# Moving one accumulating transfer ahead of two others in GpSimd's queue (gated mix of an S5 scan and an H3 convolution)

## The chip, the cores and the metric

The kernel runs on one core of a Trainium2 chip. A core has five instruction streams: TensorE (PE, matrix products into PSUM), VectorE (DVE), ScalarE (ACT), GpSimd (POOL) and SyncE (SP), and 16 DMA engines that serve the transfers issued from these streams. The metric is the time on the device in microseconds (us), as the median of several runs.

## The reference

Two branches share the input x (2048 steps, 1024 channels) and are mixed by a gate. Branch A is a diagonal complex state-space recurrence (S5); branch B shifts and multiplies two inputs and convolves the product with one long filter per channel, by FFT (H3).

```python
def _A_ref(x, Lambda_re, Lambda_im, B_re, B_im, C_re, C_im, log_dt, Dskip):
    dt = jnp.exp(log_dt)
    Lam_bar = jnp.exp(dt * Lam)
    B_bar = ((Lam_bar - 1.0) / Lam)[:, None] * Bmat
    Bu = jnp.einsum("bld,pd->blp", x + 0j, B_bar)
    for t in range(L):
        h = Lam_bar[None, :] * h + Bu[:, t, :]
        hs.append(h)
    y = 2.0 * jnp.einsum("blp,dp->bld", hseq, Cmat).real + x * Dskip[None, None, :]

def _B_ref(q, k, v, shift_k, ssm_k, ssm_D):
    for t in range(ks):                       # ks = 4 taps
        k_shift = k_shift + k_pad[:, t:t + S, :] * shift_k[:, ks - 1 - t][None, None, :]
    kv = k_shift * v
    y = irfft(rfft(kv padded) * rfft(ssm_k padded))[:S]
    y = y + kv * ssm_D[None, None, :]
    return q * y                              # q is x

g = sigmoid((x * gate_w).sum(-1, keepdims=True))
return g * a + (1 - g) * b
```

## The kernel before

The program is one unrolled list of instructions per engine; small helpers (`mm`, `tt`, `ts`, `act`, `move`, `gather`, lines 92 to 127) append each instruction to its engine's list in exactly the order of the calls, so an engine executes what the source names in that order, and waits by semaphore where its data or its buffer is not ready. `gather` is a DMA issued from POOL that adds its source to its destination; `move` and `load_t` are issued from SP. Since all helpers record their instructions at one place, nearly every instruction of the profile stands at line 94.

Branch B comes first. The 1024 channels are cut into eight groups of 128, and a loop over c = 0 to 6 (line 1136) works on three groups at a time: group c + 2 is loaded and gets its four taps, group c + 1 is transformed, group c is multiplied, and group c - 1 is transformed back. The pieces are generators; `step` runs one up to its next `yield`, `run` to its end. Those that matter here:

- `products(c)` (line 680) multiplies the spectra of filter (K) and signal (V) block by block on DVE. After its second product, `n1` into the tile `wkh`, it issues `gather(G[:, :, 1:], n1)`, 768 KB that are added into the spectrum G (line 708); a later step on DVE, `tt(G[:, :, 2:], G[:, :, 2:], n1, ALU.add)` (line 726), reads and writes G again.
- `times_v(c + 1)` (line 593) multiplies the tap sums `ks` by v, mirrors them on PE, takes a difference on DVE into `ev` and issues `gather(ks[:, 2:4], lo)`, 256 KB (line 606). `fwd_V` (line 667) reads `ev` and then `ks` on PE.
- `turn_table(c - 1)` (line 461), for c = 1 to 4, makes a piece of the tables `TC`, `TS` of cosines and sines with which branch A's scan later turns its states. It has three parts: four ACT instructions write two halves of the tile `hr` (float32 `h`, int32 `n`); `gather(h, n)` adds the second half to the first, 256 KB (line 470); three ACT instructions take the absolute value, sine and cosine. In the loop the third part comes one pass later: the generator is kept as `old`, and the next pass begins with `step(old)`.
- `inverse(c - 1)` (line 738) reads G on PE, and SP stores the result.
- `taps(c + 2)` (line 563) multiplies on PE the transposed input `kT` and a rearranged copy `kB`, which SP's transfers `spread` (line 224) prepare from c = 3 on.

Alongside, PE begins with the products of branch A (`Bu`, the generator `parts`). The tiles `hr` and the products' `t` share one pool of three buffers (`u4`, line 83). Behind the loop come the last groups of branch B, and then branch A's scans on DVE, its output products on PE and the mix with branch B.

Of the kernel before, what the change touches and what calls it, by code (L numbers as in the profile page):

```python
# [20 lines left out]
def kernel(  # L21
# [158 lines left out]
    def hold(column):  # L180
        act(column, pih, func=ACT.Copy)

    def by_channel(c):
        return c == 0 or 3 <= c < NC - 1

    def load(which, c, held=False):
        cc = slice(c * 128, (c + 1) * 128)
        if which == "kn":

            if by_channel(c):  # L190
                t = ld.tile([128, S], BF16, name="kn", tag="ld")
                move(t, B_ssm_k[cc, :])
            else:
                t = ld.tile([128, NT, 128], BF16, name="kn", tag="ld")
                load_t(t, B_ssm_k[cc, :])
        elif which == "v":

            w = 2 if c == 2 else 1
            if c == NC - 1:
                t = ld.tile([128, NT, 128], BF16, name="v", tag="ld")  # L200
            elif c == 2:
                lds["v2"] = xt_pool.tile([128, NT, 2, 128], BF16, name="v2", tag="xT")
            if c < 2:
                t = ld.tile([128, NT, 128], BF16, name="v", tag="ld")
            elif c < NC - 1:
                t = lds["v2"][:, :, c % 2:c % 2 + w].rearrange("p n k d -> p n (k d)")
            if held:
                hold(t[:, 0, 0:1])
            move(t, vf.rearrange("(n p) d -> p n d", p=128)[:, :, c * 128:(c + w) * 128])
            for k in range(w):  # L210
                lds["v", c + k] = t[:, :, k * 128:(k + 1) * 128]
            return
        else:

            t = ld.tile([128, PAD + S], BF16, name="kT", tag="ld")
            put("pool", nc.gpsimd.memset, t[:, 0:PAD], 0.0)
            if held:
                hold(t[:, PAD:PAD + 1])
            load_t(t[:, PAD:], kf[:, cc])
            if c >= 3:  # L220
                lds["kB", c] = ld.tile([128, PAD + S], BF16, name="kB", tag="ld")
        lds[which, c] = t

    def spread(c):

        a, b = lds["kT", c], lds["kB", c]
        lo, hi, n = slice(0, 64), slice(64, 128), PAD + S
        move(b[lo, 8:], a[hi, 8:])
        move(b[hi, 10:], a[hi, 8:n - 2])
        yield  # L230
        move(a[hi, 10:], a[lo, 8:n - 2])
# [13 lines left out]
    def load_BT(g, c, held=False):  # L245
        if held:
            hold(BT[g][:, c, 0, 0:1])
        load_t(BT[g][:, c], (A_B_re, A_B_im)[c][g * 256:(g + 1) * 256, :])

    def load_xT(tb, halves=(0, 1), held=False):  # L250
        if tb not in xTs:
            xTs[tb] = (xt_pool if tb in (1, 2) else xt_first).tile([128, ND, TB], BF16, name="xT", tag="xT")
        for h in halves:
            if held:
                hold(xTs[tb][:, 0, h * HB:h * HB + 1])
            load_t(xTs[tb][:, :, h * HB:(h + 1) * HB], xf[tb * TB + h:(tb + 1) * TB:2, :])
# [306 lines left out]
    def taps(c, dg):  # L563
        kT, kB = lds.pop(("kT", c)), lds.pop(("kB", c), None)
        ks = ks_pool.tile([128, 4, 4, 128], BF16, name="ks")
        for h in range(2):
            sums = tap_sums(kT, dg, h) if c < 3 else packed_sums((kT, kB), dg, h)
            act(of_blocks(ks, h), by_block(sums), func=ACT.Copy)
        kss[c] = ks
# [59 lines left out]
    def fwd_K(c, fis=range(NFI)):  # L629
        eo = eos["k", c]  # L630
        if c not in KH:
            KH[c] = spectrum("K", c)
        for fi in fis:
            fsl = slice(fi * 128, (fi + 1) * 128)
            ps = ps2([128, 2, 4, 128], "psk")
            for cc in range(2):
                tab = CF if cc == 0 else SF
                for mt in range(2):
                    mm(ps[:, cc], tab[:, mt, fsl], eo[:, cc, mt], mt == 0, c == NC - 1 and mt == 1)
                for mt in range(0 if c == NC - 1 else 2):  # L640
                    tb2 = (SF, NCF)[cc][:, mt, fsl]
                    mm(ps[:, cc, 1:4], tb2, eo[:, 1 - cc, mt, 0:3], False, mt == 1)
            act(of_tile(KH[c], fi), ps, func=ACT.Copy)
# [423 lines left out]
    def step(gen):  # L1067
        next(gen, None)

    def run(gen):  # L1070
        for _ in gen:
            pass

    def steps(gen, n):
        for _ in range(n):
            step(gen)
# [59 lines left out]
    for c in range(NC - 1):  # L1136
        n, nn = c + 1, c + 2
        if c == 0:
            load("kn", 2)
            load("kT", 2)  # L1140
            load("v", 2)
            load_BT(0, 0)
            load_xT(0, (0,))
            p1 = products(0, 1)
            fwd_K(n, (0, 1))
            step(p0)
            run(tv)
            dg = dgs(nn, True)
            steps(p1, 2)
            step(p0)  # L1150
            step(p1)
            run(p0)
            taps(nn, dg)
            step(sp)
            fwd_K(n, (2, 3))
            step(p1)
            step(sp)
            fwd_V(n)
            run(p1)
            run(fold_K(nn))  # L1160
            tv = times_v(nn)
            step(tv)
            load("kn", 3)
            load("kT", 3)
            load_BT(0, 1)
            apart = spread(3)
            step(apart)
            load_xT(0, (1,))
            run(apart)
            lam_diag(0, lam_pool, True)  # L1170
            continue
        if c == 6:
            put("pool", nc.gpsimd.tensor_copy, stamp, xTs[2][:, 0, 0:HB + 1:HB])
        tabs, back, prod = turn_table(c - 1) if c <= NG else none, inverse(c - 1), products(c)
        step(old)
        step(tabs)
        if c == 6:
            step(parts)
        step(back)
        step(tv)  # L1180
        steps(prod, 3)
        run(tv)
        step(old)
        step(tabs)
        run(back)
        run(old)
        fk = none
        if nn < NC:
            dg = dgs(nn)
            if by_channel(nn):  # L1190
                fk = fold_columns(nn)
                step(fk)
        if c == 2:
            step(parts)
        fwd_K(n, (0, 1))
        if c in (2, 6):
            step(parts)
        fwd_K(n, (2, 3))
        if c == 4:
            step(parts)  # L1200
        if c == 6:
            run(sp)
            s5p["Q"] = s5p["wu"]
            run(turns_U[2])
            gate(0)
        step(prod)
        if nn < NC:
            if not by_channel(nn):
                fk = mirror_K(nn)
            step(fk)  # L1210
            if c < 5:
                step(fk)
            if c == 4:
                step(parts)
            if c == 1:
                load_BT(1, 0, True)
            elif c < 5:
                load("v", nn, True)
            step(parts)
            taps(nn, dg)  # L1220
            if c == 5:
                load("v", nn)
                load_xT(2, held=True)
            if nn + 1 < NC:
                load("kT", nn + 1, True)
                load("kn", nn + 1)
                apart = spread(nn + 1)
                step(apart)
                if c == 1:
                    load_BT(1, 1)  # L1230
                elif c in (2, 3):
                    load_xT(1, (3 - c,))
                run(apart)
        step(prod)
        run(fk)
        run(prod)
        if n == NC - 1:
            overlap_K(n)
        if nn < NC:
            tv = times_v(nn)  # L1240
            step(tv)
            step(parts)
        else:
            run(next(tiles))
            CT[0] = ld.tile([128, 2, D], BF16, name="CTa", tag="ld")
            hold(CT[0][:, 0, 0:1])
            load_CT(0)
            load_BT(2, 0)
            load_BT(2, 1)
            run(next(tiles))  # L1250
            run(next(tiles))
        fwd_V(n, (0, 1))
        if c < 6 and c != 4:
            step(parts)
            if c in (1, 3):
                step(parts)
        fwd_V(n, (2, 3))
        if c in (4, 5):
            step(parts)
        if c == 1:  # L1260
            lam_diag(1, lam_pool)
        old = tabs
# [284 lines left out]
```

## Time and profile before

| what | value |
|---|---|
| median of 3 runs | 382.79 us (381.41 to 388.19) |
| profiled execution | 381.05 us |
| its span, first to last instruction | 379.3 us |
| PE busy | 372.4 us (98% of the span) |
| DVE busy | 369.3 us (97%) |
| ACT busy | 309.1 us (81%) |
| POOL busy | 81.2 us (21%) |
| TensorE clock granted, mean | 0.998 |
| loop passes c = 1 to 4 | about 45.9 to 139 us |

The span is one execution as the hardware profiler recorded it. The times of a table of instructions are in us from its start. A transfer has two times: its issue, which is an instruction of the issuing engine, and its landing, which the rows of the DMA issues give in us from the issue. POOL's instructions include those issues; a name such as `G<-wkh` reads "G written from wkh".

### The profile page before, as it was taken

The numbers are of one execution on the slowest core, as the hardware profiler recorded it, in microseconds if no ns is written. First come the engines' busy times: TensorE is split into PE (matmuls) and PEld (weight loads), VectorE is DVE, ScalarE is ACT, GpSimd is POOL, SyncE is SP. The second block draws the span as 40 slices with busy tenths as digits, with TensorE's granted clock in tenths as the row PEclk, the third lists the DMA queues.
The fourth block names the chain that finished last, engine by engine and source line by source line (L and its number), as shares of the span: only waits on it lengthen the run. The fifth ranks groups of instructions, "written<-read, shape, count | busy, mean of one in ns | idle before, by whom it ended". The sixth has DMA issues, their size and how long they took to land.

```text
span 379.3 us, 6708 instructions
## 1 busy us (share of the span) xinstructions
PE 372.4 (98%) x2469; PEld 200.1 (53%) x2469; DVE 369.3 (97%) x595; ACT 309.1 (81%) x475; POOL 81.2 (21%) x111
## 2 busy tenths in 40 slices
PE   7999999999999999999999999999999999999996
PEld 5656357575674846644454444444445444444444
DVE  8899999999999999999999999999999999999996
ACT  5879997988979999786949999996989759937611
POOL 4011030110301103031003112122414323635000
PEclk9999999999999999999999999999999999999999
DMA  7979999999999998969998999957898999899902
GB/s 168 168 115 242 234 202 193 232 209 202 194 170 213 233 207 177 174 144 152 199 200 188 200 230 257 250 111 134 155 231 174 221 251 246 145 250 164 225 2 111
DMA packets 126547, 71.78 MB, mean 189 GB/s; under 512 B 104681, under 2 KB 107633, under 8 KB 126514
## 3 DMA queue, kind: packets, MB, share of 16 engines
q1 hardware_dynamic: 112416, 45.90, 55.7%
q0 software_dynamic: 12976, 25.17, 39.2%
q10 hardware_dynamic: 1122, 0.28, 0.5%
q8 instruction: 19, 0.31, 0.3%
q14 instruction: 14, 0.11, 0.1%
HBM read 15.48 MB, written 8.39 MB: 63 GB/s over the span
## 4 chain that ended last, share of the span: by engine, by line
DVE 42%; PE 27%; DMA 14%; issue 10%; ACT 4%; POOL 2%; SPq 0%; DVEq 0%; POOLq 0%; ACTq 0%
PE both L94 16%; DVE BT L94 12%; DMA U<-Q 10%; DVE wkh L94 8%; DVE G L94 5%; DVE W L94 3%; PE psk L94 3%; PE psz L94 2%; DMA V<-Q 2%; DVE t L94 2%; DVE ks L94 2%; DVE hb L94 2%; PE psv L94 2%; PE taps L94 1%; DMA kT<-in_B_k_dram 1%
## 5 line engine op out<-in xcount | busy, mean ns | idle before, releaser
L94 PEld LDWEIGHTS <-BT 128*128 128x128 bf16 x640 | 62.1, 98 | 48.3 <-issue 0.2
L94 PE MATMUL both<-xT,BT 128*128 128x512 bf16 x384 | 83.7, 379 | 0.0
L94 POOL DMA_DIRECT2D U<-Q x26 | 26.4, 1029 | 82.3 <-ACT Q L94 40.5
L94 PEld LDWEIGHTS <-hb 128*128 128x128 bf16 x256 | 25.0, 98 | 30.2 <-issue 0.5
L94 PEld LDWEIGHTS <-U 128*128 128x128 bf16 x252 | 24.6, 98 | 27.4
L94 PE MATMUL psy<-CT,hb 128*128 128x512 bf16 x160 | 36.8, 379 | 0.0
L94 ACT ACTIVATE Vh<-psv 128x1024 bf16<-128x1024 f32 x32 | 30.7, 1032 | 5.8 <-PE psv L94 5.8
L94 PE MATMUL psy<-CT,U 128*128 128x512 bf16 (+1 forms) x160 | 35.1, 368 | 0.0
L94 ACT ACTIVATE U<-both 128x512 bf16<-128x512 f32 x44 | 24.2, 594 | 10.0 <-PE both L94 9.7
L94 DVE TENSOR_TENSOR_SCAN W<-rv,init,A 128x256 bf16<-128x256 f32 x48 | 32.1, 729 | 0.0
L94 POOL DMA_DIRECT2D G<-wkh x8 | 9.8, 1219 | 102.6 <-DVE wkh L94 102.6
L94 ACT ACTIVATE Q<-U,lam 128x512 bf16<-128x512 bf16 (+1 forms) x52 | 29.9, 612 | 0.0
L94 PE MATMUL psk<-eok,SF 128*128 128x384 bf16 (+1 forms) x120 | 28.5, 354 | 0.0
L94 PEld LDWEIGHTS <-SF 128*128 128x128 bf16 x184 | 18.0, 98 | 18.8 <-issue 0.2
L94 PE MATMUL psz<-G,CI 128*128 128x512 bf16 x64 | 24.3, 379 | 0.0
L94 PE MATMUL psz<-G,SI 128*128 128x512 bf16 x64 | 24.3, 379 | 0.0
L94 PE MATMUL psy<-CTa,hb 128*128 128x512 bf16 x96 | 22.7, 379 | 0.0
L94 PE MATMUL taps<-dg,kT 128*128 128x128 bf16 (+1 forms) x352 | 21.7, 210 | 0.7 <-DMA kT<-in_B_k_dram 0.6
L94 PEld LDWEIGHTS <-kT 128*128 128x128 bf16 x352 | 21.1, 100 | 2.3 <-DMA kT<-in_B_k_dram 1.8
L94 DVE TENSOR_TENSOR wkh<-BT,Vh 128x3072 bf16<-128x3072 bf16 (+4 forms) x20 | 21.8, 1109 | 0.0
L94 DVE TENSOR_TENSOR wkh<-Kh,Vh 128x3072 bf16<-128x3072 bf16 (+2 forms) x16 | 21.3, 1349 | 0.0
L94 PE MATMUL psy<-CTa,U 128*128 128x512 bf16 (+1 forms) x92 | 20.8, 370 | 0.0
(230 smaller groups left out, 843.5 us busy)
## 6 DMA issues: line engine op xcount, KB each, us to landing
U<-Q POOLq DMA_DIRECT2D x26, 256.0 KB, 5.1
G<-wkh POOLq DMA_DIRECT2D x6, 768.0 KB, 8.8
cv_scr<-cv SPq DMA_DIRECT2D x16, 256.0 KB, 7.7
kn<-in_B_ssm_k_dram SPq DMA_DIRECT2D x5, 512.0 KB, 4.4
v<-in_B_v_dram SPq DMA_DIRECT2D x5, 512.0 KB, 7.1
out_dram<-m SPq DMA_DIRECT2D x8, 256.0 KB, 4.2
BT<-cv_scr SPq DMA_DIRECT2D x7, 256.0 KB, 6.6
out_dram<-BT SPq DMA_DIRECT2D x7, 256.0 KB, 2.0
```

Of the source, the lines that this page charges most:

```text
L94: i = f(*a, **kw)
```

## The change

In the loop, `step(tabs)`, which issues `gather(h, n)`, moves up by four calls. It stood behind `run(tv)`, that is behind the transfer into `ks`; it now stands ahead of `steps(prod, 3)`, that is ahead of the transfer into G. Both orders come after the first `step(tabs)`, whose ACT instructions write `hr`. It concerns the passes c = 1 to 4; in the passes 5 and 6 `tabs` is empty.

```diff
         step(back)
         step(tv)
+        step(tabs)
         steps(prod, 3)
         run(tv)
         step(old)
-        step(tabs)
         run(back)
         run(old)
```

The lists of PE, DVE, ACT and SP keep their instructions and their order. In POOL's list each of the four passes changes from

```
G<-wkh, ks<-lo, hr<-hr
```

to

```
hr<-hr, G<-wkh, ks<-lo
```

and the clearing of a few columns of the next `kT`, which POOL does in each pass behind these, keeps its place behind `ks<-lo`. POOL's instruction for `hr<-hr` now carries a wait on ACT's writes of `hr` itself; before, waits of earlier POOL instructions had covered it.

## The prediction

> **What bounds the kernel now.** I read the page's first line, then a table of busy time over the stretch in which the moved transfer occurs, 45.9 to 139 us: four passes of the channel loop, c = 1 to 4.
>
> ```profile
> span 379.3 us, 6708 instructions
> ```
>
> ```profile
> core 0: us, PE busy (x) PEld busy (x) DVE busy (x) ACT busy (x) POOL busy (x), PEclk, DMA share, GB/s
> 45.90:139.00 93.10, 92.54 (x801) 59.62 (x802) 92.69 (x84) 84.12 (x134) 12.38 (x16) 1.00 1.07 206
> ```
>
> Of 93.10 us PE is idle for 0.56 and DVE for 0.41, at full clock. Both are full at once, so no order of transfers can take more than about half a microsecond out of these passes, while a transfer that comes late for either of them lengthens the pass at once. The DMA engines are full too (share 1.07). POOL has 12.38 us of work: its own time is worth nothing, the moments at which its transfers land are all that matters. So I follow three transfers per pass, all in POOL's queue.
>
> **The order and the landings before.** First POOL's instructions in order of time (start, duration, instruction, and in brackets what it waited for), then for the four passes in turn the rows of the DMA issues (size, and us from issue to landing).
>
> ```profile
> 50.07 1.20 POOL L94 DMA_DIRECT2D G<-wkh  x1 [14.72 <-DVE wkh L94]
> 52.88 0.91 POOL L94 DMA_DIRECT2D ks<-lo  x1 [1.61 <-DVE ev L94]
> 53.45 1.22 POOL L94 DMA_DIRECT2D hr<-hr  x1
> ...
> 74.06 1.20 POOL L94 DMA_DIRECT2D G<-wkh  x1 [18.18 <-DVE wkh L94]
> 76.87 0.90 POOL L94 DMA_DIRECT2D ks<-lo  x1 [1.61 <-DVE ev L94]
> 77.43 1.22 POOL L94 DMA_DIRECT2D hr<-hr  x1
> ...
> 97.07 1.20 POOL L94 DMA_DIRECT2D G<-wkh  x1 [15.90 <-DVE wkh L94]
> 99.88 0.90 POOL L94 DMA_DIRECT2D ks<-lo  x1 [1.61 <-DVE ev L94]
> 100.44 1.23 POOL L94 DMA_DIRECT2D hr<-hr  x1
> ...
> 120.08 1.20 POOL L94 DMA_DIRECT2D G<-wkh  x1 [17.11 <-DVE wkh L94]
> 122.89 0.90 POOL L94 DMA_DIRECT2D ks<-lo  x1 [1.60 <-DVE ev L94]
> 123.44 1.23 POOL L94 DMA_DIRECT2D hr<-hr  x1
> ```
>
> ```profile
> ks<-lo POOLq DMA_DIRECT2D x1, 256.0 KB, 8.4
> hr<-hr POOLq DMA_DIRECT2D x1, 256.0 KB, 11.1
> ```
>
> ```profile
> ks<-lo POOLq DMA_DIRECT2D x1, 256.0 KB, 7.2
> hr<-hr POOLq DMA_DIRECT2D x1, 256.0 KB, 8.5
> ```
>
> ```profile
> ks<-lo POOLq DMA_DIRECT2D x1, 256.0 KB, 7.9
> hr<-hr POOLq DMA_DIRECT2D x1, 256.0 KB, 11.6
> ```
>
> ```profile
> ks<-lo POOLq DMA_DIRECT2D x1, 256.0 KB, 8.8
> hr<-hr POOLq DMA_DIRECT2D x1, 256.0 KB, 9.9
> ```
>
> Start plus landing time gives when ks is complete: 61.28, 84.07, 107.78 and 131.69 us; and hr: 64.55, 85.93, 112.04 and 133.34. The difference is what hr takes behind ks: 3.27, 1.86, 4.26 and 1.65 us, on average 2.76. Against those landings stand the first uses. The rows are the first matmul pair on ks in each pass, the first and the last of the four additions into G on DVE, and the landing times of the four G transfers (shortest, median, longest).
>
> ```profile
> 62.04 0.59 PE L94 MATMUL psv<-ks,SF 128*128 128x512 bf16 x2
> ...
> 87.24 0.59 PE L94 MATMUL psv<-ks,SF 128*128 128x512 bf16 x2
> ...
> 109.04 0.59 PE L94 MATMUL psv<-ks,SF 128*128 128x512 bf16 x2
> ...
> 133.94 0.59 PE L94 MATMUL psv<-ks,SF 128*128 128x512 bf16 x2
> ```
>
> ```profile
> 61.77 1.23 DVE L94 TENSOR_TENSOR G<-G,wkh 128x2048 bf16<-128x2048 bf16 x1
> ...
> 131.77 1.23 DVE L94 TENSOR_TENSOR G<-G,wkh 128x2048 bf16<-128x2048 bf16 x1
> ```
>
> ```profile
> DMA to landing us min/median/max: 8.8/8.9/9.2
> ```
>
> ks has 0.76, 3.17, 1.26 and 2.25 us to spare. G was used 11.70 us after its issue in the first pass and 11.69 in the last; with the longest landing, 9.2, that leaves 2.49 to spare. Neither made anyone wait. hr has more than that: its next reader is the ScalarE instruction below, 3.86 us after the landing at 64.55.
>
> ```profile
> 68.41 0.63 ACT L94 ACTIVATE hr<-hr 128x512 f32<-128x512 f32 x1
> ```
>
> **The change, part by part.** No instruction is added or removed. One POOL issue per pass with its 256 KB DMA moves, from behind ks to ahead of G. PE, DVE, ACT and SP keep their order.
>
> *What it removes.* hr no longer stands last in POOL's queue. Nobody waited for it there, and PE and DVE have 0.56 and 0.41 us of idle time in all; worth between 0 and 0.56 us, taken as 0, because hr lands well ahead of its reader.
>
> *The wait on POOL.* hr must now wait for ScalarE to have written both halves of it, with G's issue queued behind on POOL, and ks behind G. The last writes are these; POOL's lag after a release is read from the DVE row, whose product ends at 49.78 while G's issue starts at 50.07: 0.29 us.
>
> ```profile
> 47.26 0.90 ACT L94 ACTIVATE hr<-row,nthn 128x256 int32<-128x256 f16 x2
> ...
> 70.86 0.90 ACT L94 ACTIVATE hr<-row,nthn 128x256 int32<-128x256 f16 x2
> ...
> 94.43 0.93 ACT L94 ACTIVATE hr<-row,nthn 128x256 int32<-128x256 f16 x2
> ...
> 117.86 0.89 ACT L94 ACTIVATE hr<-row,nthn 128x256 int32<-128x256 f16 x2
> ```
>
> ```profile
> 48.03 1.75 DVE L94 TENSOR_TENSOR wkh<-Kh,Vh 128x3072 bf16<-128x3072 bf16 x1
> ```
>
> They end at 48.16, 71.76, 95.36 and 118.75; with the lag, hr is issued at 48.45, 72.05, 95.65 and 119.04, ahead of G's old starts by H = 1.62, 2.01, 1.42 and 1.04 us. hr's issue takes 1.22 us, so only in the last pass can G be pushed on POOL itself, by up to 0.19 us. hr's own issue comes 5.00, 5.38, 4.79 and 4.40 us earlier than before.
>
> *The queue of the DMA engines.* In every pass G, ks and hr landed in the order of issue, so I take POOL's queue as first in, first out: hr's 256 KB are now served before G. If hr needs S us of service, it delays G and then ks by D = S - H. S is not shown at this place. From below: 1.65 us, the smallest of the four spacings; from above 4.26, the largest. I take the mean, 2.76. Then D is 1.14, 0.75, 1.34 and 1.72 us. G's 2.49 us cover all of it. ks's cover holds in the second and fourth pass and falls short by 1.14 - 0.76 = 0.38 and 1.34 - 1.26 = 0.08 in the first and third: PE then waits in front of the ks matmuls, everything of PE behind it, and DVE's next products soon after. Sum: 0.46 us, put down as **0.5 us slower**. With S = 1.65 the sum is 0. With S = 4.26, D is 2.64, 2.25, 2.84 and 3.22; ks is late by 1.88, 0, 1.58 and 0.97 = 4.43 us, and G by 0.15, 0, 0.35 and 0.73 at most, which lies beside the same stalls for the most part; I take 5 us as the end.
>
> The Trainium skill, "DMA: Bandwidth & Descriptors", section "Anatomy of one DMA — SWDGE (gpsimd) path", gives about 2.0 us fixed plus bytes over 436 GB/s for such a transfer, by which 256 KB occupy the engines for an estimated 0.6 us: the sum by it is 0. The spacings of 1.65 to 4.26 us say that this queue never gets the engines alone here.
>
> *Neighbours in the other queue.* hr now moves while SP's transfers for the next taps do. The tightest one is in the fourth pass:
>
> ```profile
> 121.21 0.47 SPq L94 DMA_DIRECT2D kT<-kT  x1
> ```
>
> ```profile
> kT<-kT SPq DMA_DIRECT2D x1, 256.8 KB, 7.4
> ```
>
> ```profile
> 129.90 0.22 PE L94 MATMUL taps<-dg,kT 128*128 128x64 bf16 x2
> ```
>
> It landed at 128.61, 1.29 us ahead of the taps. What POOL's queue takes more than before is the head start H, 1.04 us in this pass, so even a delay of that length would still be covered: 0.
>
> **The sum.** It is made against the profiled execution, 381.05 us (379.3 of span and 1.75 around it). The median of the runs shown is 382.79, 1.74 above it, with runs from 381.41 to 388.19; the new kernel will be measured by such runs too, so I add to the median: 382.79 + 0.5 = **383.3 us**. Something like 2% (7.7 us) is what a measurement of this kernel can tell from no change.
>
> **The rivals.**
>
> 1. *ks late in earnest, still inside 2%.* If each pass keeps its own spacing (3.27 and 4.26 in the first and third), D is 1.65 and 2.84, and ks is late by 0.89 and 1.58: 2.5 us, 385.3. A middle value comes from the share of the engines:
>
> ```profile
> q0 software_dynamic: 560, 1.31, 34.3%
> ```
>
> In the first pass (45.9 to 69 us) POOL's queue filled 34.3% of the 16 engines, 7.92 us for 1280 KB, so 1.58 us per 256 KB. If the other queue is full as well and the two take turns, S is twice that, 3.17; D is 1.55 and 1.75 in the passes that matter, and ks is late by 0.79 and 0.49: 1.3 us, 384.1. That the engines take turns between queues packet by packet is the rule of the Trainium skill, same page, "Queues, rings and completion order"; no row here shows single packets. For this rival: the DMA share of 1.07. Against: G landed within 8.8 to 9.2 us in all passes, whatever was beside it.
>
> 2. *Slower by more than 2%: hr holds the head of the queue.* Place: hr's transfer of 32-bit words, in front of G in POOL's queue. Price: with S = 5.3 us, D is 3.7, 3.3, 3.9 and 4.3, ks is late by 2.9, 0.1, 2.6 and 2.0, together 7.7 us: 390.5. From S = 5.3 on it decides, and each further microsecond costs four. For it: hr's 11.1 and 11.6 us to landing are the longest of the three transfers. Against: most of that is waiting behind ks, and no spacing exceeds 4.26.
>
> 3. *Faster.* POOL's queue is empty 1.7 to 4.3 us sooner in each pass, so the next loads of SP go undisturbed. The gain is capped by PE's 0.56 us of idle time: 382.2. More than 2% faster would need a stretch in which PE and DVE are not full; this one has none.
>
> 4. *The change moves nothing.* If ScalarE wrote hr later than DVE finishes the product for G, hr's issue would sit at G's place and hold G back. The writes end 1.3 to 2.3 us ahead of G's issue in all four passes, so the order really changes; if it did not, G's issue would slip by hr's 1.22 us at most, within its 2.49: 382.8.
>
> **How the numbers follow.** The forecast (0 to about 1 us slower) has 0.60, rival 1 0.20, rival 2 0.12, rival 3 0.05 (of which 0.03 past 2%), rival 4 0.03. The range goes from 381.0 (the lowest run, 381.41, less the 0.5 that can be gained) to 388.0 (the median plus the 5 us of the largest spacing). It leaves rival 2 out, and the tail of 3. Faster by over 2%: 0.03; within: 0.85; slower: 0.12.
>
> **What the new profile would show.** POOL's order hr, G, ks, with hr about 0.3 us after ScalarE's last write and G's starts unmoved within 0.2 us; hr landing about 5 us after its issue instead of 8.5 to 11.6; G and ks landing D = 0.7 to 1.7 us later after their issues than before; a PE or ScalarE wait that ends with the landing of ks in the first pass, of some tenths. The passes stay at 23 to 24 us. Wrong would be: waits of PE on ks or of DVE on G of over 2 us in each pass (rival 2), landings of G unchanged (then hr is served in the head start and S is below 1.4), or a change of the time outside 45.9 to 139 us, which nothing above provides for.

## The result

| | median of 21 runs | lowest and highest | ratio to before, 95% interval |
|---|---|---|---|
| before | 381.68 us | 380.76 and 391.12 | |
| changed kernel | 386.88 us | 381.79 and 791.68 (the next 394.64) | 1.006 (1.0035 to 1.0086) |

The ratio stands for 1.3 to 3.3 us on 381.68: slower, within 2%. The medians differ by more because part of the executions of every kernel here, the one before and one without the moved transfer included, run 4 to 8 us longer behind 219 us (judged by a time over 385 us: 13 of these 21 of the changed kernel and 4 of 21 before, but 6 of 12 and 13 of 23 when both were measured again, so whether the change makes them more frequent is open), and the ratio still counts four of them (385.16 to 387.23 us), without which it would stand for about 1.2 us. The changed kernel's profiled execution took 387.70 us, so a second profile of the same kernel, called `again` (382.64 us), is read below; where the first one is meant it is called `after`. Stages are compared by the time between the same two issues, since the first pass begins up to 2 us earlier or later from run to run.

The table of busy time from G's issue in the first pass to its issue in the fifth, columns as in the prediction: the kernel before, then `again`.

```profile
50.07:143.09 93.02, 92.52 (x801) 59.59 (x800) 92.61 (x83) 84.04 (x132) 12.38 (x16) 1.00 1.06 204
```

```profile
49.95:144.14 94.19, 92.47 (x794) 59.76 (x800) 92.87 (x83) 83.85 (x131) 11.49 (x15) 1.00 1.02 203
```

PE and DVE do the same work, and the four passes are 1.17 us longer (0.79 in `after`, where the fifth issue comes at 143.84 after 50.03). From there to the end `again` takes 236.76 us and the kernel before 236.21. So most of the loss is made in the passes. POOL's list in order of time, and the landings of the four passes in turn:

```profile
48.33 0.89 POOL L94 DMA_DIRECT2D hr<-hr  x1 [13.10 <-ACT hr L94]
49.95 1.21 POOL L94 DMA_DIRECT2D G<-wkh  x1 [0.74 <-DVE wkh L94]
52.76 0.90 POOL L94 DMA_DIRECT2D ks<-lo  x1 [1.60 <-DVE ev L94]
73.59 0.86 POOL L94 DMA_DIRECT2D hr<-hr  x1 [17.82 <-ACT hr L94]
74.35 1.33 POOL L94 DMA_DIRECT2D G<-wkh  x1
...
97.18 0.86 POOL L94 DMA_DIRECT2D hr<-hr  x1 [14.49 <-ACT hr L94]
97.95 1.31 POOL L94 DMA_DIRECT2D G<-wkh  x1
...
120.38 0.86 POOL L94 DMA_DIRECT2D hr<-hr  x1 [16.08 <-ACT hr L94]
121.25 1.22 POOL L94 DMA_DIRECT2D G<-wkh  x1
```

```profile
G<-wkh POOLq DMA_DIRECT2D x1, 768.0 KB, 10.3
hr<-hr POOLq DMA_DIRECT2D x1, 256.0 KB, 5.9
ks<-lo POOLq DMA_DIRECT2D x1, 256.0 KB, 10.8
```

```profile
G<-wkh POOLq DMA_DIRECT2D x1, 768.0 KB, 9.6
hr<-hr POOLq DMA_DIRECT2D x1, 256.0 KB, 4.9
ks<-lo POOLq DMA_DIRECT2D x1, 256.0 KB, 8.1
```

```profile
G<-wkh POOLq DMA_DIRECT2D x1, 768.0 KB, 9.7
hr<-hr POOLq DMA_DIRECT2D x1, 256.0 KB, 4.0
ks<-lo POOLq DMA_DIRECT2D x1, 256.0 KB, 8.8
```

```profile
G<-wkh POOLq DMA_DIRECT2D x1, 768.0 KB, 10.2
hr<-hr POOLq DMA_DIRECT2D x1, 256.0 KB, 6.2
ks<-lo POOLq DMA_DIRECT2D x1, 256.0 KB, 8.8
```

hr lands 4.0 to 6.2 us after its issue (before: 8.5 to 11.6), G 9.6 to 10.3 (before: 8.8 to 9.2), and ks in the first pass 10.8 (before: 8.4). What PE waited for in the four passes is two rows, both in the first:

```profile
58.94 0.23 PE L94 MATMUL taps<-dg,kT 128*128 128x64 bf16 x2 [0.73 <-DMA kT<-kT]
63.58 0.59 PE L94 MATMUL psv<-ks,SF 128*128 128x512 bf16 x2 [0.61 <-DMA ks<-lo]
```

1.34 us of PE, more than half of it for `kT`, a transfer of SP's queue. G's issues are 24.40, 23.60, 23.30 and 22.89 us apart, against 23.99, 23.01, 23.01 and 23.01. So the second and third pass are longer too, by 0.59 and 0.29 us, though PE waits for no transfer there.

### The profile page after: what moved, and what is told of

Same layout as the page of the kernel before. It is cut to its first block, busy times and chain, and to the rows that moved or that the text cites. A ratio compares the mean times of both kernels' runs of the same rounds, so it can differ in the third digit from the quotient of the medians.

```text
span 385.9 us, 6709 instructions
## 1 busy us (share of the span) xinstructions
PE 375.3 (97%) x2469; PEld 201.5 (52%) x2469; DVE 370.1 (96%) x595; ACT 310.1 (80%) x475; POOL 81.6 (21%) x111
## 4 chain that ended last, share of the span: by engine, by line
PE 50%; DVE 29%; ACT 8%; issue 6%; DMA 6%; POOL 0%; SPq 0%; DVEq 0%; ACTq 0%; POOLq 0%
PE psy L94 29%; DVE BT L94 7%; DVE wkh L94 7%; DVE G L94 5%; PE psk L94 4%; PE both L94 4%; DVE t L94 4%; PE taps L94 3%; DMA ks<-lo 3%; PE psv L94 3%; PE foldk L94 2%; DMA CT<-in_A_C_im_dram 2%; PE odd L94 2%; PE even L94 2%; ACT Vh L94 1%
## 5 line engine op out<-in xcount | busy, mean ns | idle before, releaser
L94 ACT ACTIVATE U<-both 128x512 bf16<-128x512 f32 x44 | 24.2, 594 | 10.8 <-PE both L94 10.6
L94 PE MATMUL psy<-CTa,hb 128*128 128x512 bf16 x96 | 24.2, 398 | 2.8 <-ACT U L94 2.8
L94 PE MATMUL psk<-eok,CF 128*128 128x512 bf16 x64 | 19.4, 379 | 0.1
```

Of the source, the lines that this page charges most:

```text
L94: i = f(*a, **kw)
```

## The experiments

Two theories. By the *queue theory* of the prediction, hr delays G and ks in POOL's queue, each pass by its own amount. By its rival, the *late theory*, the passes cost little, and a shift of them makes later loads collide. The expectations call a pass by its number c, "S" and "D" as in the prediction. In the table, "passes" is the time from G's first issue to its fifth in the one profile of each kernel, less the 93.02 us of before.

| label | edit | ratio (95%) | passes, us |
|---|---|---|---|
| again | the changed kernel | 1.0045 (0.9989 to 1.0101) | +1.17 |
| twice | 256 KB more ahead of G | 1.0176 (1.0076 to 1.0275) | +4.19 |
| half | 128 KB of hr ahead of G | 1.0110 (1.0029 to 1.0191) | +1.07 |
| half2 | the same kernel again | 1.0016 (0.9972 to 1.0061) | +0.58 |
| no_hr | before, without hr's transfer | 1.0052 (0.9995 to 1.0110) | -0.01 |
| odd | hr ahead in passes 1 and 3 | 1.0033 (0.9980 to 1.0085) | +1.49 |
| even | hr ahead in passes 2 and 4 | 0.9992 (0.9949 to 1.0035) | +0.74 |
| between | hr between G and ks | 1.0070 (1.0007 to 1.0133) | +2.41 |
| pe1 | before, 1.3 us more of PE in pass 1 | 1.0049 (1.0015 to 1.0083) | +0.81 |
| only1 | hr ahead in pass 1 only | 1.0059 (1.0005 to 1.0113) | +2.31 |
| not1 | hr ahead in passes 2 to 4 | 1.0007 (0.9960 to 1.0054) | 0.00 |
| before2 | the kernel before | one run, 382.24 us | -0.01 |

### The changed kernel again, and hr left out

> The changed kernel once more, to see it undisturbed. Queue theory (hr is served ahead of G and ks, and PE waits for ks where ks had little to spare): G lands about 10 us after its issue, PE waits a few tenths to 1.2 us in the first pass, the fifth pass starts about 0.8 us later than before, and nothing else moves: 382 to 383 us, ratio 1.002 to 1.003. Late theory (the passes cost little, but a shift of them makes the loads of the output matrices behind 215 us collide): the fifth pass starts 0.8 us later and a further 1 to 5 us is lost behind 215 us, so 383 to 387 us.

The passes fit both theories in size, and behind the fifth issue 0.55 us came on top (236.76 against 236.21): the late theory's 1 to 5 us did not come in this execution. Over all profiles the stretch behind the fifth issue takes 236.2 to 236.8 us in seven and 239.9 to 244.7 us in the seven others. `only1` below, whose passes are 2.31 us longer, has 236.17, and `no_hr`, whose passes are not shifted at all, has 244.65: a shift of the passes is neither needed for the longer stretch nor enough for it, and the late theory falls. What makes the stretch longer is open.

```diff
         for o, rate in ((h, thn), (n, nthn)):
 ...
-        gather(h, n)
         yield
```

> The kernel before without hr's transfer at all (left out, so the tables are not the reference's): what hr cost at its old place. Both theories: it cost nothing that PE or DVE waited for, so 380.8 to 381.7 us, ratio 0.998 to 1.000, the four passes 0 to 0.5 us shorter in all. If it is 2 us or more faster, hr cost something at its old place that the profile does not show as a wait.

The passes take 93.01 us, to 0.01 us those of before: at its old place hr cost PE and DVE nothing. The ratio, expected at 1.000 or below, came out at 1.0052 with an interval that reaches from 0.9995 up; nothing in the passes answers to it, and in the profile the excess lies behind the fifth issue (244.65 us against 236.21). Here and in `half` and `half2` the factor of the two sines in `turn_table` is set to 1 as well; the number of instructions stays the same.

### The dose: twice and half

```diff
+    spare = dram.tile([NG, 128, 2, HB], I32, name="spare")
 ...
         gather(h, n)
+        put("pool", nc.gpsimd.dma_start, out=spare[g], in_=n)
         yield
```

> As the changed kernel, with a second transfer of 256 KB behind hr and ahead of G in every pass (the second half of hr is also copied to a scratch tensor in DRAM). Queue theory: S rises from about 2.5 to 5 us, D to 3 to 4 us; ks is late in all four passes and G in some: 6 to 9 us over the kernel before in the passes alone, G landing 12 to 13 us after its issue. Late theory: the passes get about 1 us longer than in the changed kernel, total not more than 3 us over it.

The time rises by 2.9 to 10.6 us and the passes by 4.19, of which 2.84 in the first: less than the 6 to 9 expected, and G landed in 9.6 to 10.8 us, not in 12 to 13. The direction is the queue theory's, the size is not. Behind the fifth issue this execution took 244.0 us against 236.2, so only a part of its time over the kernel before is made in the passes.

```diff
-        gather(h, n)
+        gather(h[:, 0], n[:, 0])
         yield
```

> As the changed kernel, but hr's transfer adds only one of the two halves, 128 KB (the other half is left out, so the tables are not the reference's). Queue theory: S is about 1.3 us, less than the head start of 1.0 to 2.0 us, so ks is not late: the passes as in the kernel before, 381 to 382 us, ratio 1.000. Late theory: the same in the passes, and also no loss behind 215 us, since nothing shifts; if the total stays 2 us or more over the kernel before although the fifth pass starts on time, the place of the issue itself costs, not the size.

This expectation failed. The passes were 1.07 us longer, and PE waited 1.61 us for ks. Run again:

> The kernel with 128 KB of hr ahead of G again. Queue theory as first stated (half the bytes, no loss): the passes as in the kernel before. If the first pass is again 0.3 us or more longer with PE waiting for ks, the bytes ahead of G are not what decides in the first pass, and it is which of the neighbouring transfers the early issue meets.

```profile
62.59 0.59 PE L94 MATMUL psv<-ks,SF 128*128 128x512 bf16 x2 [0.90 <-DMA ks<-lo]
```

PE waited for ks once more, 0.90 us, although G was on time (8.5 us to landing; before: 9.2) and ks alone was late (10.2; before: 8.4). A plain queue in which hr goes first would delay G as much as ks. So something else came between. (The first interval between G's issues is 23.98 us, as before; the 0.58 us appear in the next two.) The rows of the two large DMA queues (packets, MB moved, and share of 16 engines, in 2 us) show what changed: q0 is POOL's queue, q1 SP's. First the 2 us from G's issue in the first pass, of the kernel before and of `again`:

```profile
q1 hardware_dynamic: 1872, 0.48, 120.9%
```

```profile
q1 hardware_dynamic: 891, 0.29, 77.2%
q0 software_dynamic: 37, 0.08, 28.2%
```

Then the 2 us that begin 4 us after G's issue, in the same order:

```profile
q0 software_dynamic: 119, 0.37, 99.2%
q1 hardware_dynamic: 17, 0.02, 4.0%
```

```profile
q0 software_dynamic: 92, 0.28, 72.5%
q1 hardware_dynamic: 653, 0.23, 46.8%
```

In the kernel before, SP's queue has the engines to itself up to 2 us behind G's issue, and from 4 to 6 us nearly all that moves is G. With hr early, SP's queue moves less in the first window: 0.24 to 0.37 MB in the seven profiles with hr, or half of it, ahead of G in the first pass, against 0.47 to 0.51 in the six in which it is not (`before`, `before2`, `not1`, `no_hr`, `even`, `pe1`). The two queues together fall too, to 0.33 to 0.40 MB, so SP's queue loses more than POOL's gains; why is open. The second window separates less: 0.03 MB of SP's queue (`only1`) to 0.24 (`half`) with hr early, 0.02 to 0.16 without. By the order of SP's issues it is the transposed load of x, issued 2 to 3 us ahead of G, that falls behind, and after it the copy into kT. In `again` SP's queue was some 0.5 us behind already when hr was issued (its copies into kB came 3.36 us ahead of G's issue, 3.91 to 4.35 in the six); in `only1`, which loses the most with 256 KB ahead, it was not (4.09).

That this is also why the ks of `half2` was late with G on time is an inference from these rows; single packets were not seen, and kT was on time for PE there.

### Which pass pays

```diff
+        if c in (1, 3):        # odd; even: (2, 4); only1: (1,); not1: (2, 3, 4)
+            step(tabs)
         steps(prod, 3)
         run(tv)
         step(old)
-        step(tabs)
+        if c not in (1, 3):
+            step(tabs)
```

> hr ahead of G in the first and third pass only, where ks had 0.76 and 1.26 us to spare. Queue theory: nearly all of the change's loss: the fifth pass starts 0.6 to 1 us later, 382 to 383 us. Late theory: the same shift, and a further 1 to 5 us behind 215 us.

> hr ahead of G in the second and fourth pass only, where ks had 3.17 and 2.25 us to spare. Queue theory: no loss, the fifth pass starts within 0.2 us of the kernel before, 381 to 382 us, ratio 1.000. Late theory: no shift and so no loss behind 215 us either. A loss of 1 us or more here would speak for a cost of the place itself, with G or ks on time.

`odd` lost 1.49 us in the passes, G's issues 24.72, 23.60, 23.18 and 23.01 us apart. `even` lost nothing in the first three (23.98, 23.01, 23.00) and 0.76 in the fourth, where PE waited for the transposed load of x:

```profile
PE even L94 <- DMA xT<-in_A_x_dram: 1.1, 1, 1.1
```

Again a transfer of SP's queue, not ks; the expectation of no loss in `even` failed. `odd` suggested a third theory: the cost is made in the first pass, and what is seen in the second and third is its echo. `pe1` shows the echo by itself, and `only1` and `not1` test the theory:

```diff
+        if c == 1:
+            idle = ps2([128, 2, 512], "idle")
+            for k in range(6):
+                mm(idle[:, 0], SF[:, 0, 0:128], CF[:, 0], True, True)
         fwd_V(n, (0, 1))
```

> The kernel before, with six matmuls of 512 columns (0.216 us apart, 1.3 us in all) whose result nobody reads, put on PE ahead of the first ks matmuls of the first pass: a shift of about 1.3 us without any transfer moved. Queue theory: the shift is all, 382 to 383 us, ratio 1.002 to 1.004, and the stretch behind 215 us takes as long as before. Late theory: this shift brings the later loss too, and the times spread as those of the changed kernel do, up to 387 us.

No transfer is moved here; PE alone is 1.3 us later, once. G's issues:

```profile
49.67 1.20 POOL L94 DMA_DIRECT2D G<-wkh  x1 [14.72 <-DVE wkh L94]
73.71 1.20 POOL L94 DMA_DIRECT2D G<-wkh  x1 [18.23 <-DVE wkh L94]
97.31 1.20 POOL L94 DMA_DIRECT2D G<-wkh  x1 [15.26 <-DVE wkh L94]
120.49 1.20 POOL L94 DMA_DIRECT2D G<-wkh  x1 [16.84 <-DVE wkh L94]
143.50 1.20 POOL L94 DMA_DIRECT2D G<-wkh  x1 [14.96 <-DVE wkh L94]
```

They are 24.04, 23.60, 23.18 and 23.01 us apart: nearly nothing in the first interval, 0.59 and 0.17 in the next two. These are the figures of `odd`, and of `again` to 0.12 us. A PE that is late in the first pass passes it on to DVE later: ScalarE writes Vh from what PE has made, and in the second pass DVE waits for it.

```profile
93.05 2.29 DVE L94 TENSOR_TENSOR G<-Kh,Vh 128x4096 bf16<-128x4096 bf16 x1 [0.50 <-ACT Vh L94]
```

The lateness in the second and third pass is not made there.

> hr ahead of G in the first pass only. First-pass theory (the cost is made in the first pass, where the copy kT and ks both have little to spare, and a PE that is late there by more than about half a microsecond then has nothing left to absorb it in the second and third pass): the whole loss of the change, 0.8 to 1.5 us between G's issues of the first and the fifth pass (93.02 us before), with passes of about 24.3, 23.6, 23.2 and 23.0. Rival (each pass adds its own delay): about 0.3 us, with passes two to four as before.

> hr ahead of G in the second to fourth pass, not in the first. First-pass theory: no loss in the first three passes (23.99, 23.01, 23.01), at most some tenths in the fourth if the transposed load of x comes late there as with the second and fourth pass alone; total 381 to 382 us, ratio 0.998 to 1.002. Rival (each pass adds its own delay): 0.5 to 1 us in these three passes, 382 to 383 us.

The table of busy time from G's first issue to its fifth, `only1` and then `not1`, and below it the waits of PE, and of DVE, in the first pass of `only1`:

```profile
51.30:146.63 95.33, 92.83 (x801) 59.77 (x800) 92.86 (x83) 83.84 (x131) 11.50 (x15) 1.00 1.03 199
```

```profile
49.79:142.81 93.02, 92.52 (x802) 59.61 (x800) 92.61 (x83) 84.04 (x132) 12.30 (x17) 1.00 1.01 203
```

```profile
58.78 1.91 PE L94 MATMUL odd<-xT,BT 128*128 128x256 bf16 x16 [1.14 <-DMA xT<-in_A_x_dram]
61.99 0.23 PE L94 MATMUL taps<-dg,kT 128*128 128x64 bf16 x2 [1.30 <-DMA kT<-kT]
```

```profile
63.45 1.23 DVE L94 TENSOR_TENSOR G<-G,wkh 128x2048 bf16<-128x2048 bf16 x1 [0.49 <-DMA G<-wkh]
```

The first pass alone makes the whole loss, here 2.31 us, with 23.60, 23.19 and 23.00 behind it; the other three passes with hr ahead cost nothing in `not1`, 93.02 us to the hundredth. The first-pass theory holds for these kernels and "each pass adds its own" falls. The fourth pass can lose as well, as `even` showed, but did not in `not1`, with hr at the same place there. The size of the first pass's loss varies between executions: `after` 0.79, `again` 1.17, `odd` 1.49, `only1` 2.31 us. The second profile of the kernel before asks whether its own passes vary too:

> The kernel before once more, for a second profile: passes of 23.99, 23.01, 23.01 and 23.01 us as in the first one, and ks on time, if these do not vary from run to run. If the first pass varies by half a microsecond in the kernel before too, the single profiles of the others say less.

They do not: 23.99, 23.01, 23.01 and 23.00 us, in an execution whose first pass began 1.17 us later than in the first profile.

### hr behind G

```diff
-        step(tabs)
         steps(prod, 3)
+        step(tabs)
         run(tv)
```

> hr issued behind G and ahead of ks. Queue theory: G is not delayed; ks is, by all of S less the 1.5 us that POOL idles between G and ks only if the queue is empty then, which it is not, so by about 2 to 3 us: PE waits about 1.5 to 2 us in the first pass, 1 in the third, 0 to 0.5 in the fourth: 3 us over the kernel before, so worse than the change. Late theory: 1 us in the passes and a further 1 to 5 behind 215 us, as with the change.

```profile
64.65 0.59 PE L94 MATMUL psv<-ks,SF 128*128 128x512 bf16 x2 [2.74 <-DMA ks<-lo]
```

G landed as before (9.4 us) and ks 12.0 us after its issue in place of 8.4: PE waited 2.74 us, in the first pass only (the wait expected in the third did not come), and the passes were 2.41 us longer. Here hr is in front of ks with no head start, and ks is 3.6 us later: the order inside POOL's queue does count, and S for this place is, by estimate, about 3.6 us.

### How late PE is, and what it costs

Eight profiles can now be read together. Before, the first `psv<-ks` of the first pass starts 11.97 us after G's issue (62.04 - 50.07), and the first `taps<-dg,kT`, which is ahead of it on PE, 7.93 us after (58.00); the second profile of the kernel before gives the same two figures. The rows of `psv<-ks` in `after`, `odd`, `only1`, `half` and `pe1`, in this order; those of `again`, `half2` and `between` stand above:

```profile
63.21 0.59 PE L94 MATMUL psv<-ks,SF 128*128 128x512 bf16 x2 [0.18 <-DMA ks<-lo]
64.77 0.59 PE L94 MATMUL psv<-ks,SF 128*128 128x512 bf16 x2
66.07 0.59 PE L94 MATMUL psv<-ks,SF 128*128 128x512 bf16 x2
65.30 0.59 PE L94 MATMUL psv<-ks,SF 128*128 128x512 bf16 x2 [1.61 <-DMA ks<-lo]
62.94 0.59 PE L94 MATMUL psv<-ks,SF 128*128 128x512 bf16 x2
```

| label | taps later by, us | ks matmuls later by, us | passes longer by, us |
|---|---|---|---|
| half2 | 0 | 1.06 | 0.58 |
| after | 0.82 | 1.21 | 0.79 |
| pe1 | 0 | 1.30 | 0.81 |
| half | 0 | 1.56 | 1.07 |
| again | 1.06 | 1.66 | 1.17 |
| odd | 1.94 | 1.98 | 1.49 |
| only1 | 2.76 | 2.80 | 2.31 |
| between | 0 | 2.90 | 2.41 |

Whatever made PE late, a transfer or six idle matmuls, the passes get longer by that lateness less 0.48 to 0.49 us (0.42 in `after`). So the loss of the passes is PE's lateness at its ks matmuls of the first pass. With all of hr ahead of G, most of it is there at the taps already, that is ahead of ks: the profile names kT in all four (in `after` in front of a weight load), and the load of x in `only1`. (In `odd` a further 1.02 us is put down to ScalarE's `eok`, which runs there 6.21 us after G's issue, as before at 6.22, so it was not ScalarE that was late.) With half of hr, or with hr between G and ks, it is ks alone. `even` and `twice` lost time in the fourth and the third pass too and are not in the table.

## Why the prediction was right, and where it was not

- **What bounds it: right.** `not1` and `no_hr` show that neither taking hr out nor moving it in three passes makes the four passes shorter by more than 0.01 us: nothing was to be gained.
- **The wait on POOL: right.** In `again` ScalarE's last write of the first pass ends at 48.03, and hr's issue follows at 48.33. Where PE is not late (`not1`), hr starts 2.00, 1.41 and 1.02 us ahead of G in the second to fourth pass; the prediction had 2.01, 1.42 and 1.04. In `again` itself hr was 0.76 to 0.87 us ahead there, because ScalarE, which follows PE, was late too.
- **The queue of the DMA engines: right in size for G in `again`, only partly for ks.** There G's landings rose by 1.1, 0.8, 0.7 and 1.4 us against a forecast D of 1.14, 0.75, 1.34 and 1.72, and those of ks by 2.4, 0.9, 0.9 and 0; DVE did not wait for G. PE waited for ks 0.61 us in the first pass (forecast 0.38), and not in the third (forecast 0.08). In the first pass of `odd` and `only1` G was 2.5 and 2.9 us later, at the end of its cover of 2.49, and DVE waited 0.49 us for it in `only1`. S was taken from spacings of landings behind ks, 2.76 on average; `between` gives about 3.6. And first in, first out was not the whole mechanism, as `half2` shows.
- **Neighbours in the other queue, priced at 0: the step that failed.** The prediction took the fourth pass's kT as the tightest and allowed it the head start H. For the first pass's kT and load of x the profile before gives no landing, and the prediction did not look at them. They were late in their turn: PE waited 0.73 us for kT in `again`, 2.44 for both in `only1`. hr's early service comes out of SP's queue, and the delay of that queue is not bounded by H: with H = 1.62 us in the first pass, the taps were 0.82 to 2.76 us late.
- **The sum over the passes: wrong in form.** Adding up each pass's own lateness gave 0.46 us. Measured were 0.79 and 1.17, all from PE's lateness in the first pass, and most of it appears only in the intervals of the second and third (in `after` the first interval is 23.99 us, as before). The size is near rival 1's middle value, 1.3, by another path: luck.
- **Rivals.** Rival 2 (over 2%) did not come; even 256 KB more gave 1.0176 (1.0076 to 1.0275), which does not quite rule out 2% for that kernel. Rival 3 is excluded by `no_hr` and `not1` as far as the passes go. Rival 4: the order did change.
- **The time.** The range, 381.0 to 388.0 us, holds the measured median of 386.88, but in part by luck: `after` took 5.85 us more than before behind the fifth issue (242.06 against 236.21) and 0.79 in the passes, and the prediction provided for nothing there; it named a change of the time outside the passes as a sign of being wrong. Whether the change has a part in it is open. The ratio stands for 1.3 to 3.3 us, above the 0.5 forecast and around rival 1's 1.3 and 2.5. The four profiles with 256 KB ahead of G in the first pass lost 0.79 to 2.31 us in the passes, 1.44 on average, which reaches into the interval from below. Why the first pass's lateness differs so much between executions stays open.

## What to carry to other kernels

Here the DMA engines were full (share 1.06), and a transfer issued earlier took its time out of what the other queue was moving at that moment (0.24 to 0.37 MB in 2 us in place of 0.47 to 0.51). Where that is so, look for the first use of those transfers too, in every pass, not only for those behind it in its own queue. A loop's passes need not have the same cover, and a late engine can pay in a later pass than the one that made it late; compare the interval between the same issue from pass to pass before adding up.

## What the runs showed of the hardware that was not expected

Half the bytes ahead of G, which should have fitted into the head start, did not take the delay away: `half` and `half2` lost 1.07 and 0.58 us in the passes, the full 256 KB 0.79 to 2.31, and a further 256 KB 4.19. The two DMA queues together moved fewer bytes with hr early, 0.33 to 0.40 MB in the 2 us from G's issue in place of 0.47 to 0.51. And 6 matmuls on PE in one pass, 1.3 us, cost 0.05 us in that pass's interval and 0.76 in the next two.
